# Weights from float64 with three instead of four word operations, and two factor groups with earlier due times

## The chip, the cores and the metric

The kernel runs on one core of a Trainium2 chip. The metric is the device time of one launch in microseconds. Before the change it is 1022.02 us, the median of three runs (1018.5 to 1025.15).

## The reference

Causal attention with a decay (4 batches, 8 heads, 576 positions, head dimension 64) gives 2304 tokens of width 512. Two layers of the same kind follow, each with a weight of 512 x 2048 and one of 2048 x 512 and a nonlinearity between them. Cut to what matters:

```python
scores = np.matmul(q, k.transpose(0, 1, 3, 2)) / np.sqrt(D) + decay      # causal, then softmax
x = attention @ v                                                        # (2304, 512)
h = x @ moe_w_in;  x = (h * np.clip(h + 3, 0, 6) / 6) @ moe_w_out
h = x @ moe2_w_in; g = np.maximum(h, 0) + np.log1p(np.exp(-np.abs(h)))
out = g @ moe2_w_out
```

The four weights reach the kernel as float64, since they are drawn as float64 and scaled. It reads each number as two 32-bit words and makes a float32 of it on the chip.

## The kernel before

**Stages.** Attention works on pairs of heads, 16 in all, for four batches. The first MoE starts on the first 512 tokens as soon as the first batch is through, so that attention and the first three token blocks of the first MoE (its matmuls are L1299 and L1362) run interleaved up to about 480 us. The last two token blocks follow, together with the making of the second MoE's weights and factors, up to about 645 us. The second MoE is done by a scheme with seven products in place of eight: phase A (L1415) makes its hidden layer in steps and sends it to DRAM, phase B (L1516) reads it back, makes factors of it (factors_g) and multiplies them with the second weight. At the border of the phases, about 825 to 860 us, both overlap.

**Weights.** There are 64 weight pieces of 128 x 512 numbers: 32 for the first MoE, whose result goes on to W tiles (L1035 on ScalarE takes the high part, L1036 on GpSimd the rest), and 32 for the second, most of which are written to DRAM as float32 and read again later. raw_weights brings one piece in by a DMA of 512 KB into a staging tile st, with low and high words side by side, and turns it into float32. Of the high word, seen as a float32, the exponent is shifted by a multiplication with 2 to the power -112 (conv0, on ScalarE at L1017, or on VectorE at L1016). The low word is shifted right by 29 (conv1, L1019). Then the high word shifted left by 3 is or-ed with that (conv2, L1020), and last the sign bit of the high word is or-ed in (conv3, L1023). The last three run on VectorE (DVE), and conv2 needs conv0.

**Order.** All operations are first recorded, each with the engine or engines that may do it (with a price in ns), what it reads and writes, and a due time `at` in us. Work.order then lists them: engine by engine it takes, of the operations that could start now, the one with the earliest due time. Where two engines may do an operation, it goes to the one that would be through with it first by the prices. So a removed operation moves nearly everything behind it by some places. The result is a fixed order for each engine; at run time an engine waits where an operand is late. Loads and stores stand in SP's order.

In factors_g and for the last weight group of the second MoE (weights2_in with p = 7), the due times counted from the phases' planned starts are:

```python
at = mb_at(t, 2 * d) - 7
weights2_in(1, p, ma_at(t, p, 1) + 4, 2)
```

Of the kernel before, what the change touches and what calls it, by code (L numbers as in the profile page):

```python
# [10 lines left out]
U32 = mybir.dt.uint32  # L11
ACTF = mybir.ActivationFunctionType
ALU = mybir.AluOpType
# [36 lines left out]
    pc=794.25,  # L50
# [21 lines left out]
    cvw=29.86,  # L72
# [33 lines left out]
class Work:  # L106
# [11 lines left out]
    def op(self, ways, fn=None, r=(), w=(), after=(), at=0.0, banks=(), hold=(), free=(), nbytes=0, name="", seq=None, from_=0.0, rows=1.0):  # L118


        o = Op()
        o.ways = [ways] if isinstance(ways, tuple) else list(ways)
        o.at, o.banks, o.hold, o.free, o.nbytes, o.name = at, list(banks), hold, free, nbytes, name
        o.deps, o.succ, o.est, o.eng = {}, [], 1000.0 * from_, None
        o.early, o.rows = self.mark, rows
        for b in o.banks:
            b.users += 1
        r, w = list(r) + o.banks, list(w)
        for t in r:
            if t in self.writer:  # L130
                o.deps[self.writer[t]] = 1
        for t in w:
            for d in [self.writer.get(t)] + self.readers.get(t, []):
                if d is not None:
                    o.deps.setdefault(d, 1)
        for t in after:
            for d in [self.writer.get(t)] + self.readers.get(t, []):
                if d is not None:
                    o.deps.setdefault(d, 0)
        if seq:  # L140
            if seq in self.writer:
                o.deps.setdefault(self.writer[seq], 0)
            self.writer[seq] = o
        for t in r:
            self.readers.setdefault(t, []).append(o)
        for t in w:
            self.writer[t] = o
            self.readers[t] = []
        self.ops.append(o)
        return o  # L150
# [123 lines left out]
def attention_two_moe_kernel(  # L274
# [18 lines left out]
    nc = tc.nc  # L293
# [15 lines left out]
    K = PLAN  # L309
# [27 lines left out]
    def act(n, psum, extra=0):  # L337
        return 0.833 * n + (50 if psum else 93) + 93 * extra

    def dve(n, fast=False, extra=0):  # L340
        return (0.52 if fast else 1.04) * n + 67 + 61 * extra
# [30 lines left out]
    def ma_at(t, p, x=0.0):  # L372

        return M2_0 + K["SA"] * (t * NPR + p + x)

    def mb_at(t, p, x=0.0):

        return MB + K["SB"] * (t * NPR + p + x)
# [606 lines left out]
    def words(i):  # L985

        return staging(i).bitcast(F32).rearrange("p n e -> p (n e)").rearrange("p (e n) -> p e n", e=2)

    def raw_weights(i, m, o, ft, at, dense=False):

        def load():
            dst = staging(i).rearrange("p n e -> p (n e)")
            if not wide:
                dst = dst.bitcast(F32)[:, 0:NC * P]
            if o == 0:
                dst = dst.rearrange("p (c f) -> p c f", c=NC)  # L1000
            nc.sync.dma_start(out=dst, in_=w_source(m, o, ft))

        dma(load, 8 * P * NC * P, w=[("stage", i), ("up", i)] + [("o", i, 0), ("o", i, 1)] * (i < 2), r=["m2"] * (i in (2, 3)), at=at - K["ldw"], name="loadw", from_=K["wfrom"])

        def up():
            return staging(i)[:, :, 1]

        def upf():
            return up().bitcast(F32)

        def low():
            return staging(i)[:, :, 0]

        n = NC * P
        if wide:
            op([("dve", dve(n, True), lambda: nc.vector.tensor_scalar(upf(), upf(), 2.0 ** -112, None, op0=ALU.mult), K["pc"]),  # L1016
                ("act", act(n, False), lambda: nc.scalar.activation(out=upf(), in_=upf(), func=ACTF.Copy, scale=2.0 ** -112))],  # L1017
               w=[("up", i)], at=at - K["cvw"], name="conv0")
            op(("dve", dve(n, True), lambda: nc.vector.tensor_scalar(low(), low(), 29, None, op0=ALU.logical_shift_right)), w=[("stage", i)], at=at - K["cvw"], name="conv1")  # L1019
            op(("dve", dve(n), lambda: nc.vector.scalar_tensor_tensor(  # L1020
                out=low(), in0=up(), scalar=3, in1=low(), op0=ALU.logical_shift_left, op1=ALU.bitwise_or,
            )), r=[("up", i)], w=[("stage", i)], at=at - K["cvw"], name="conv2")
            op(("dve", dve(n), lambda: nc.vector.scalar_tensor_tensor(  # L1023
                out=words(i)[:, 0].bitcast(U32) if dense else low(), in0=up(), scalar=0x80000000, in1=low(), op0=ALU.bitwise_and, op1=ALU.bitwise_or,
            )), r=[("up", i)], w=[("stage", i)] + [("up", i)] * dense, at=at - K["cvw"], name="conv3")

    def weights(o, ft, at):

# [115 lines left out]
    def weights2_in(o, p, at, i0):  # L1144

        def dst(z0, z1):
            return lambda s: unit_w(p).rearrange("p s z f -> p s (z f)")[:, s, z0 * 2 * P:z1 * 2 * P]

        weights2(o, p, at, [(a, b, dst(a, b), [("unit2" if o else "unit", p)], lambda: None) for a, b in ((0, 4), (4, 6), (6, 7))], i0)
# [319 lines left out]

    def factors_g(t, d):  # L1470

        at = mb_at(t, 2 * d) - 7
        i = (t * NPR // 2 + d) % 2
        raw = st[i].rearrange("p n e -> p (n e)").bitcast(F32)
        rv = raw.rearrange("p (r f h n) -> p r f h n", r=2, f=2, h=2)

        def cv():
            return (GT if i else BIG["XT"])[:, 0:8 * P].rearrange("p (z r n) -> p z r n", z=4, r=2)

        a0, a1 = t * NG, (t + 1) * NG  # L1480
        dma(lambda: nc.sync.dma_start(out=raw.rearrange("p (f s) -> p f s", f=4), in_=g_dram[4 * d:4 * d + 4, :, a0:a1].rearrange("f p s -> p f s")),
            16 * P * NG, r=[("gd", x, y) for x in range(a0 // NA, (a1 - 1) // NA + 1) for y in (2 * d, 2 * d + 1)],
            w=[("stage", i), ("up", i)], at=at - 8, name="loadg")
        A11, A12, A21, A22 = (rv[:, :, f, h] for h in range(2) for f in range(2))
        for x, (u, v, sub) in enumerate(((A21, A22, False), (0, A11, True), (A11, A21, True), (A12, 1, True))):
            def go(e, x=x, u=u, v=v, sub=sub):
                u, v = (cv()[:, y] if isinstance(y, int) else y for y in (u, v))
                e.tensor_tensor(cv()[:, x], u, v, op=ALU.subtract if sub else ALU.add)
            op(either(2 * P, go, 300), r=[("stage", i)] + [("C", i, y) for y in (u, v) if isinstance(y, int)], w=[("C", i, x)], at=at, name="gS")
        for n, z0, z1, src, rd in ((4 * P, 0, 2, lambda: rv[:, :, :, 0].rearrange("p r f n -> p f r n"), [("stage", i)]), (2 * P, 2, 3, lambda: A22, [("stage", i)]),  # L1490
                                   (8 * P, 3, 7, cv, [("C", i, x) for x in range(4)])):
            def dst(s, z0=z0, z1=z1):
                return gops(i, s)[:, z0:z1] if z1 > z0 + 1 else gops(i, s)[:, z0]

            op(("act", act(n, False), lambda src=src, dst=dst: nc.scalar.activation(out=dst(0), in_=src(), func=ACTF.Copy)),  # L1495
               r=rd, w=[("gf", i, z0, 0)], at=at + 1, name="gfh")

            def lo(e, src=src, dst=dst):
                e.tensor_tensor(dst(1), src(), dst(0).bitcast(F32), op=ALU.subtract)  # L1499
            op(either(n, lo, 300), r=rd + [("gf", i, z0, 0)], w=[("gf", i, z0, 1)], at=at + 1, name="gfl")  # L1500
# [107 lines left out]
    for t in range(NTA):  # L1608
        for p in range(NPR):
            step_a(t, p)  # L1610
            if p == NPR - 2 and t + 1 < NTA:
                factors_x(t + 1, ma_at(t, 1), 5.0)
            if t == NTA - 1:
                if p < 2:
                    freed([("xf", (t - 1) % 2, f) for f in AT[2]], [("unit2", p)])
                    freed([("unit", p)], [("gf", p, z0, s) for z0 in (0, 2, 3) for s in range(2)])
                else:
                    freed([("unit", p)], [("unit2", p)])
                if p < NPR - 1:
                    load_wo(p, ma_at(t, 0) if p < 2 else ma_at(t, p, 1))  # L1620
                else:
                    freed([("H", 0, q) for q in range(4)] + [("Yt", 0, 0), ("Yt", 0, 1)], [(x, i) for x in ("stage", "up") for i in (2, 3)])
                    weights2_in(1, p, ma_at(t, p, 1) + 4, 2)
    freed([("xt", 0), ("xt", 1)], [("C", 0, x) for x in range(4)])
    freed([("stage", 4), ("up", 4)], [("C", 1, x) for x in range(4)])
    freed([("stage", 5), ("up", 5)], [("u", x) for x in range(3)])
# [45 lines left out]
```

## Time and profile before

| | |
|---|---|
| median of three runs | 1022.02 us (1018.5 to 1025.15) |
| the profiled execution | 1020.33 us |
| its span, first to last instruction | 1018.3 us |
| TensorE (PE) busy | 978.4 us, 96% of the span |
| VectorE (DVE) busy | 838.2 us, 82% |
| ScalarE (ACT) busy | 599.8 us, 59% |
| GpSimd (POOL) busy | 256.4 us, 25% |
| mean granted TensorE clock | 0.993 |

A busy share is a mean over stages with different limits. PE's busy time is modelled from pipelined matmuls, so that a PE without idle time may still not be at its peak; its idle time is what tells of waits. The time outside the span, 2.0 us, belongs to the start and the end of the launch.

### The profile page before, as it was taken

The page shows a single profiled execution, that of the slowest core. Times are in us where ns is not written, and L with a number is a line of the kernel's source. Part 1 is how long each engine was busy: PE and PEld are TensorE (multiplying, and loading weights), DVE is VectorE, ACT ScalarE, POOL GpSimd, SP SyncE. Part 2 cuts the span into 40 slices and gives each one's busy share as a digit, 9 for nine tenths or more (in the row PEclk, how much of TensorE's full clock was granted, in tenths as well). Part 3 has the DMA queues.
Part 4 walks back from the last instruction along what each step waited for, and adds up shares of the span by engine and source line. Part 5 has one row for each costly group of instructions (what it writes and reads, how often), then busy time and mean ns, then how long its engine had stood idle before and what let it go on. Part 6 is the DMA issues. An engine that isn't in the chain of part 4 may idle for free.

```text
span 1018.3 us, 17717 instructions
## 1 busy us (share of the span) xinstructions
PE 978.4 (96%) x6116; PEld 850.4 (84%) x6116; DVE 838.2 (82%) x1662; ACT 599.8 (59%) x1309; POOL 256.4 (25%) x245
## 2 busy tenths in 40 slices
PE   8999999889999999999999999999999999999997
PEld 6566677668788888888888778899999999999997
DVE  8789979998999868998676878787787758888885
ACT  6899766877667557675443545665555544443442
POOL 2221241220000010000345744210010308454442
PEclk9999999999999999999999999999999999999999
DMA  6666553445545526443565660554324994444342
GB/s 138 168 143 157 136 145 94 122 134 153 145 141 144 135 66 177 118 138 104 180 209 178 225 212 21 163 169 141 140 105 164 340 359 134 126 146 145 112 125 77
DMA packets 192066, 153.47 MB, mean 151 GB/s; under 512 B 108220, under 2 KB 163932, under 8 KB 191080
## 3 DMA queue, kind: packets, MB, share of 16 engines
q1 hardware_dynamic: 191976, 152.34, 50.2%
q8 instruction: 48, 0.79, 0.3%
q14 instruction: 42, 0.34, 0.1%
HBM read 99.68 MB, written 52.47 MB: 149 GB/s over the span
## 4 chain that ended last, share of the span: by engine, by line
PE 67%; DVE 19%; issue 5%; ACT 3%; DMA 3%; POOL 2%; SPq 1%; DVEq 0%; POOLq 0%; ACTq 0%
PE bank L1516 16%; PE bank L1415 15%; PE bank L1299 13%; PE bank L1362 13%; PE bank L685 4%; PE bank L846 3%; PE bank L776 3%; DVE MX L1322 2%; DVE st L1020 2%; DVE GT L1341 1%; DVE st L1023 1%; DVE p L701 1%; DMA st<-in_moe_w_in_dram 1%; DVE KB L632 1%; DVE QA L632 1%
## 5 line engine op out<-in xcount | busy, mean ns | idle before, releaser
L1299 PE MATMUL bank<-MX,W 128*128 128x512 f32 x768 | 225.4, 406 | 4.1 <-DVE GT L1341 2.9
L1362 PE MATMUL bank<-MX,W 128*128 128x512 f32 (+1 forms) x688 | 188.4, 382 | 3.5 <-DVE MX L1322 3.5
L1299 PEld LDWEIGHTS bank<-MX,W 128*128 128x128 f32 x768 | 133.7, 191 | 26.6 <-DVE GT L1341 3.9
L1362 PEld LDWEIGHTS bank<-MX,W 128*128 128x128 f32 x688 | 121.6, 189 | 25.5 <-DVE MX L1322 4.1
L1516 PE MATMUL bank<-rW,rW 128*128 128x256 f32 x1134 | 138.6, 283 | 1.3 <-POOL rW L1139 0.9
L1516 PEld LDWEIGHTS bank<-rW,rW 128*128 128x128 f32 x1134 | 136.9, 191 | 2.1 <-POOL rW L1139 1.1
L1415 PE MATMUL bank<-XO,rW 128*128 128x288 f32 x672 | 92.7, 298 | 2.2 <-DVE HY L1433 1.6
L1415 PEld LDWEIGHTS bank<-XO,rW 128*128 128x128 f32 x672 | 90.3, 188 | 4.0 <-DVE HY L1433 2.3
L710 ACT ACTIVATE p<-p,stats 64x64 f32<-64x64 f32 (+4 forms) x130 | 72.2, 556 | 27.8 <-DVE stats L701 26.9
L1495 ACT ACTIVATE rW<-st 128x512 fp32r<-128x512 f32 (+1 forms) x72 | 36.9, 518 | 76.9 <-PE bank L1516 46.5
L1036 POOL TENSOR_TENSOR W<-st,W 128x512 fp32r<-128x512 f32 x24 | 34.9, 1456 | 159.8 <-ACT W L1035 133.8
L1339 ACT ACTIVATE GT<-bank,three 128x512 f32<-128x512 f32 x80 | 51.3, 643 | 39.6 <-DVE MX L1322 18.1
L1415 PE MATMUL bank<-MX,rW 128*128 128x288 f32 x480 | 70.2, 297 | 1.0 <-DVE HY L1433 1.0
L1415 PEld LDWEIGHTS bank<-MX,rW 128*128 128x128 f32 x480 | 65.7, 188 | 1.8 <-DVE HY L1433 1.4
L776 PE MATMUL bank<-ident,p 128*128 128x128 f32 x390 | 58.6, 275 | 8.3 <-DVE xs L861 4.4
L776 PEld LDWEIGHTS bank<-ident,p 128*128 128x128 f32 x390 | 46.2, 140 | 23.9 <-DVE xs L861 4.4
L581 POOL TENSOR_TENSOR V<-vr,V 128x640 fp32r<-128x640 f32 x10 | 17.2, 1718 | 189.3 <-ACT V L577 189.3
L811 ACT ACTIVATE pth<-bank 128x320 fp32r<-128x320 f32 (+2 forms) x100 | 42.3, 433 | 37.4 <-PE bank L776 26.3
L1322 DVE TENSOR_TENSOR MX<-GT,MX 128x512 fp32r<-128x512 f32 (+1 forms) x69 | 51.9, 757 | 13.0 <-ACT MX L1319 12.3
L1499 POOL TENSOR_TENSOR rW<-st,rW 128x256 fp32r<-128x256 f32 (+1 forms) x35 | 41.1, 1178 | 80.8 <-ACT rW L1495 66.5
L1341 DVE SCALAR_TENSOR_TENSOR GT<-GT,bank 128x512 f32<-128x512 f32 x80 | 49.8, 628 | 13.1 <-ACT GT L1339 12.5
L701 DVE CUSTOM_DVE_ANT_0 p<-bank,bar 64x64 f32<-64x64 f32 (+4 forms) x130 | 51.9, 421 | 6.4 <-PE bank L685 5.8
(220 smaller groups left out, 2102.8 us busy)
## 6 DMA issues: line engine op xcount, KB each, us to landing
st<-g_dram SPq DMA_DIRECT2D x36, 512.0 KB
st<-in_moe_w_out_dram SPq DMA_DIRECT2D x32, 512.0 KB
st<-in_moe_w_in_dram SPq DMA_DIRECT2D x30, 512.0 KB
wo_dram<-XO SPq DMA_DIRECT2D x49, 256.0 KB
g_dram<-HY SPq DMA_DIRECT2D x16, 576.0 KB
g_dram<-rBW SPq DMA_DIRECT2D x16, 576.0 KB
rW<-wo_dram SPq DMA_DIRECT2D x5, 1792.0 KB
wf_dram<-st SPq DMA_DIRECT2D x24, 256.0 KB
```

Of the source, the lines that this page charges most:

```text
L701: nc.vector.tensor_tensor_reduce(out=T["P"][par][ti][:r, a:c], in0=bank[bk.i][:r, o:o + c - a], in1=bar[:r, b0:b0 + c - a], op0=ALU.add, o ...
L710: nc.scalar.activation(out=pt, in_=pt, func=ACTF.Exp, scale=-1.0, bias=sv[:r, 0, ti:ti + 1], accum_out=sv[:r, 1, ti:ti + 1],)
L776: nc.tensor.transpose(acc[:, p0:p0 + P], T["P"][par][ti][:, k0:k0 + P], ident)
L811: nc.scalar.activation(out=place("PTH", j, ks, a, c), in_=src(), func=ACTF.Copy)
L1299: nc.tensor.matmul(bank[bk.i][:, 0:n], w[:, c], x[:, c, 0:n], start=(c == 0 and p == 0), stop=(c == NC - 1 and p == 2))
L1322: op(("dve", dve(n), lambda: nc.vector.tensor_tensor(t(glt), g, t(ght).bitcast(F32), op=ALU.subtract)), r=[("g", i), ("gh", i3)], w=[("gl" ...
L1339: op(("act", act(n, True, 1), lambda: nc.scalar.activation(out=g, in_=bank[bk.i][:, 0:n], func=ACTF.Relu, bias=three)), r=["three"], banks ...
L1341: op(("dve", dve(n), lambda: nc.vector.scalar_tensor_tensor(out=g, in0=g, scalar=6.0, in1=bank[bk.i][:, 0:n], op0=ALU.min, op1=ALU.mult)), ...
L1362: nc.tensor.matmul(bank[b][:, o:o + n], w[:, c * P:(c + 1) * P], x, start=(ft == 0 and p == 0 and o == 0), stop=(ft == NF - 1 and p == 2), ...
L1415: nc.tensor.matmul(bank[bks[b].i][:, 0:HA], wa[u][:, c], xa[v][:, c], start=(nm in ("P1", "P2", "P5") and c == 0 and y == 0), stop=(c == 1 ...
L1499: e.tensor_tensor(dst(1), src(), dst(0).bitcast(F32), op=ALU.subtract)
L1516: nc.tensor.matmul(bank[bks[b].i][:, o * 256:(o + 1) * 256], ga[u], wa[v], start=(p == 0 and o == 0 and y == 0), stop=(p == NPR - 1 and y ...
```

## The change

conv0 becomes one ScalarE activation with the function Prelu, the same scale and a slope of -(2 to the power 32) for negative numbers. A negative high word thus comes out positive, with an exponent that is higher by 32, and the shift left by 3 in conv2 carries that bit to the place of the sign. So conv3 goes, and conv2 writes the result where conv3 did. The choice of VectorE for conv0 goes too. At the border, the first two factor groups of phase B get a due time that is earlier by 18 us and the last weight group one that is later by 9 us.

```diff
--- before.py
+++ after.py
@@ -992,6 +992,7 @@
 
 
 
+
         def load():
             dst = staging(i).rearrange("p n e -> p (n e)")
             if not wide:
@@ -1013,16 +1014,12 @@
 
         n = NC * P
         if wide:
-            op([("dve", dve(n, True), lambda: nc.vector.tensor_scalar(upf(), upf(), 2.0 ** -112, None, op0=ALU.mult), K["pc"]),
-                ("act", act(n, False), lambda: nc.scalar.activation(out=upf(), in_=upf(), func=ACTF.Copy, scale=2.0 ** -112))],
+            op(("act", act(n, False), lambda: nc.scalar.activation(out=upf(), in_=upf(), func=ACTF.Prelu, scale=2.0 ** -112, alpha=-(2.0 ** 32))),
                w=[("up", i)], at=at - K["cvw"], name="conv0")
             op(("dve", dve(n, True), lambda: nc.vector.tensor_scalar(low(), low(), 29, None, op0=ALU.logical_shift_right)), w=[("stage", i)], at=at - K["cvw"], name="conv1")
             op(("dve", dve(n), lambda: nc.vector.scalar_tensor_tensor(
-                out=low(), in0=up(), scalar=3, in1=low(), op0=ALU.logical_shift_left, op1=ALU.bitwise_or,
-            )), r=[("up", i)], w=[("stage", i)], at=at - K["cvw"], name="conv2")
-            op(("dve", dve(n), lambda: nc.vector.scalar_tensor_tensor(
-                out=words(i)[:, 0].bitcast(U32) if dense else low(), in0=up(), scalar=0x80000000, in1=low(), op0=ALU.bitwise_and, op1=ALU.bitwise_or,
-            )), r=[("up", i)], w=[("stage", i)] + [("up", i)] * dense, at=at - K["cvw"], name="conv3")
+                out=words(i)[:, 0].bitcast(U32) if dense else low(), in0=up(), scalar=3, in1=low(), op0=ALU.logical_shift_left, op1=ALU.bitwise_or,
+            )), r=[("up", i)], w=[("stage", i)] + [("up", i)] * dense, at=at - K["cvw"], name="conv2")
 
     def weights(o, ft, at):
 
@@ -1469,7 +1466,7 @@
 
     def factors_g(t, d):
 
-        at = mb_at(t, 2 * d) - 7
+        at = mb_at(t, 2 * d) - (7 if t or d > 1 else 25)
         i = (t * NPR // 2 + d) % 2
         raw = st[i].rearrange("p n e -> p (n e)").bitcast(F32)
         rv = raw.rearrange("p (r f h n) -> p r f h n", r=2, f=2, h=2)
@@ -1620,7 +1617,7 @@
                     load_wo(p, ma_at(t, 0) if p < 2 else ma_at(t, p, 1))
                 else:
                     freed([("H", 0, q) for q in range(4)] + [("Yt", 0, 0), ("Yt", 0, 1)], [(x, i) for x in ("stage", "up") for i in (2, 3)])
-                    weights2_in(1, p, ma_at(t, p, 1) + 4, 2)
+                    weights2_in(1, p, ma_at(t, p, 1) + 13, 2)
     freed([("xt", 0), ("xt", 1)], [("C", 0, x) for x in range(4)])
     freed([("stage", 4), ("up", 4)], [("C", 1, x) for x in range(4)])
     freed([("stage", 5), ("up", 5)], [("u", x) for x in range(3)])
```

Lines of the changed kernel are lower by three from conv2 on (L1320 is L1317 there).

On DVE, at the last of the first MoE's 32 weight pieces (its tile is st_171; the rows around it are of attention, p and stats, and of the first MoE, GT and MX), before:

```order
L1019 TENSOR_SCALAR st_171<-st_171 128x512
L701 ISA p_152,stats_148<-bank_72,bar 64x64
L701 ISA stats_148 64x1
L1020 SCALAR_TENSOR_TENSOR st_171<-st_171 128x512
L1322 TENSOR_TENSOR MX<-GT,MX 128x512
L1023 SCALAR_TENSOR_TENSOR st_171<-st_171 128x512
L701 ISA p_153,stats_148<-bank_72,bar 128x192
L701 ISA stats_148 128x1
```

and now:

```order
L1019 TENSOR_SCALAR st_171<-st_171 128x512
L701 ISA p_153,stats_148<-bank_76,bar 128x192
L701 ISA stats_148 128x1
L701 ISA p_154,stats_148<-bank_71,bar 128x320
L701 ISA stats_148 128x1
L1020 SCALAR_TENSOR_TENSOR st_171<-st_171 128x512
L701 ISA p_155,stats_148<-bank_72,bar 128x448
L701 ISA stats_148 128x1
L1317 CAST MX<-GT 128x512
L816 TENSOR_TENSOR ptl_1439<-bank_75,pth_1435 128x320
L1319 TENSOR_TENSOR MX<-GT,MX 128x512
```

The row L1023 is gone, and between L1019 and L1020, and behind L1020, other rows stand. L1317 is one of the operations with two possible engines: it makes the high part of the first MoE's factor and stood on ACT more often before. In the whole order DVE has 64 rows of L1023 before and none now; 31 rows of L1320 before and 39 of L1317 now; 35 rows of L645 (a copy of a query or key factor, ACT or DVE) before and 39 now. On ACT the rows of L1017 are 63 before and 64 now.

On POOL at the border of the phases (XT and GT hold the sums of the factor groups, st_170 and st_171 the loaded groups, HY the last weight group), before:

```order
L1488 TENSOR_TENSOR XT<-st_170 128x256
L1488 TENSOR_TENSOR XT<-XT,st_170 128x256
L1499 TENSOR_TENSOR rW_5029<-st_171,rW_5029 128x256
L1107 TENSOR_TENSOR HY<-HY 128x256 x3
L1499 TENSOR_TENSOR rW_4877<-st_170,rW_4877 128x256
L1488 TENSOR_TENSOR GT<-st_171 128x256
L1488 TENSOR_TENSOR GT<-GT,st_171 128x256
L1488 TENSOR_TENSOR GT<-st_171,GT 128x256
L1139 TENSOR_TENSOR rW_5871<-HY,rW_5871 128x256
```

and now:

```order
L1485 TENSOR_TENSOR XT<-st_170 128x256
L1485 TENSOR_TENSOR XT<-XT,st_170 128x256
L1496 TENSOR_TENSOR rW_4973<-st_171,rW_4973 128x256
L1104 TENSOR_TENSOR HY<-HY 128x256 x3
L1496 TENSOR_TENSOR rW_4821<-st_170,rW_4821 128x256
L1485 TENSOR_TENSOR GT<-st_171 128x256
L1485 TENSOR_TENSOR GT<-GT,st_171 128x256
L1485 TENSOR_TENSOR GT<-st_171,GT 128x256
L1136 TENSOR_TENSOR rW_5809<-HY,rW_5809 128x256
```

The lines are lower by three and the tiles have other numbers; the operations stand in the same order. The same holds for every engine's order from the middle of phase A to the end: 98 rows of POOL, over 290 of ACT, over 430 of DVE, 125 DMAs of SP and all of phase B's matmuls. With the new due times at the border alone, and the four word operations as they were, the order of every engine is row by row that of before; with the three word operations alone it is row by row that of the change.

ACT's order holds two table loads before and two now, at the start and at the first softplus of phase A.

## Rows read from the trace of the kernel before

**Rows 1.** The page, first section: busy us, share of the span, instructions.

```profile
PE 978.4 (96%) x6116; PEld 850.4 (84%) x6116; DVE 838.2 (82%) x1662; ACT 599.8 (59%) x1309; POOL 256.4 (25%) x245
```

**Rows 2.** Stretches in us: length, busy us of each engine (instructions), granted clock, DMA.

```profile
0.00:50.00 50.00, 45.18 (x223) 29.71 (x224) 41.01 (x116) 36.67 (x101) 10.69 (x25) 1.00 0.69 155
50.00:100.00 50.00, 48.49 (x259) 33.06 (x258) 45.88 (x119) 46.60 (x118) 9.87 (x8) 1.00 0.65 151
100.00:250.00 150.00, 137.08 (x697) 105.94 (x695) 133.28 (x281) 108.28 (x239) 37.01 (x25) 0.98 0.48 127
250.00:475.00 225.00, 221.09 (x1205) 183.73 (x1204) 198.79 (x475) 151.53 (x351) 13.21 (x8) 1.00 0.47 133
475.00:645.00 170.00, 162.94 (x900) 138.89 (x899) 123.89 (x187) 77.03 (x167) 72.90 (x77) 0.99 0.53 167
```

**Rows 3.** PE's waits from 100 to 250 us: us in total, times, longest.

```profile
PE bank L776 <- DVE xs L861: 2.7, 2, 1.8
PE bank L1362 <- DVE MX L1322: 2.3, 1, 2.3
PE bank L776 <- DVE ptl L816: 2.2, 2, 1.2
```

**Rows 4.** The same stretches as Rows 2, instructions of L1023 alone: DVE busy.

```profile
0.00:50.00 50.00, 3.08 (x5) 1.00 0.69 155
50.00:100.00 50.00, 3.75 (x6) 1.00 0.65 151
100.00:250.00 150.00, 19.26 (x23) 0.98 0.48 127
250.00:475.00 225.00, 16.35 (x22) 1.00 0.47 133
475.00:645.00 170.00, 6.71 (x8) 0.99 0.53 167
```

**Rows 5.** Chain that ended last, by line: 100 to 250 us, then 250 to 475.

```profile
by line: PE bank L1299 15.4%; issue 9.8%; DVE st L1020 8.8%; PE bank L1362 8.7%; DVE st L1023 6.3%; DVE MX L1322 6.1%; PE bank L846 5.9%; PE bank L685 3.9%; PE bank L776 3.8%; DVE p L701 3.0%; DVE st L1019 2.7%; DVE KB L632 2.5%; DVE QA L63
...
by line: PE bank L1362 29.3%; PE bank L1299 27.4%; PE bank L685 9.9%; PE bank L776 9.0%; PE bank L846 5.0%; issue 3.7%; DVE xs L861 1.4%; DVE QA L632 1.3%; DVE KB L632 1.3%; DVE st L1020 1.2%; DVE GT L1341 0.9%; DVE MX L1281 0.8%; DVE p L70
```

**Rows 6.** The same chain, pieces from 500 to 650 us: start, us, what.

```profile
580.03 1.15 DVE st L1023
...
598.39 0.60 DVE HY L1023
...
614.44 0.61 DVE st L1023
```

**Rows 7.** L1023 over the span: count, ns least, median, most, first and last start.

```profile
L1023 DVE SCALAR_TENSOR_TENSOR st<-st x62: 630/689/1997, 22.2 to 647.7; 128x512 uint32<-128x512 uint32 x62
```

**Rows 8.** Around 187 us, DVE and POOL in order of time: start, us, engine, line.

```profile
187.42 1.80 DVE L1020 SCALAR_TENSOR_TENSOR st<-st 128x512 uint32<-128x512 uint32 x1
...
187.36 1.31 POOL L1036 TENSOR_TENSOR W<-st,W 128x512 fp32r<-128x512 f32 x1 [2.08 <-ACT W L1035]
```

**Rows 9.** Groups by form: count, busy us, mean ns, idle before and its releaser.

```profile
L1017 ACT ACTIVATE st<-st 128x512 f32<-128x512 f32 x61 | 41.1, 675 | 8.4 <-DMA st<-in_moe_w_in_dram 7.4 <-DMA st<-in_moe_w_out_dram 0.8
...
L1339 ACT ACTIVATE GT<-bank,three 128x512 f32<-128x512 f32 x64 | 43.8, 686 | 28.1 <-PE bank L1299 11.5 <-DVE MX L1322 10.1 <-DVE SB L1322 5.5
...
L1320 DVE CAST MX<-GT 128x512 fp32r<-128x512 f32 x28 | 12.9, 462 | 15.3 <-PE bank L1362 14.8
...
L645 DVE CAST QB<-QA 64x576 fp32r<-64x576 f32 x18 | 12.9, 718 | 0.1
```

**Rows 10.** The stretch from 225 to 235 us, columns as in Rows 2.

```profile
225.00:235.00 10.00, 7.72 (x26) 5.76 (x25) 7.65 (x21) 5.35 (x15) 2.81 (x2) 0.66 0.28 91
```

**Rows 11.** DVE's waits, 0 to 650 us: us in total, times, longest.

```profile
DVE st L1020 <- ACT st L1017: 3.4, 8, 1.1
```

**Rows 12.** PE's waits at the border, 822 to 860 us.

```profile
PE bank L1516 <- POOL rW L1139: 0.9, 1, 0.9
PE bank L1516 <- POOL rW L1499: 0.3, 1, 0.3
```

## Prediction

> **What bounds the kernel now.** I read the busy shares first [rows 1]: PE is busy 96% of the span, so that a gain can come only out of the few places where PE waits or runs slowly. The table of stretches [rows 2] tells where these are. From 250 to 475 us PE is idle for 225 - 221.1 = 3.9 us, from 475 to 645 us for 7.1 us. From 100 to 250 us it is idle for 150 - 137.1 = 12.9 us, and there DVE is busy 133.3 of 150 us, while ACT is busy 108.3 and POOL 37.0. The longest waits of PE in this stretch all end with DVE [rows 3]. So from 100 to 250 us DVE is a second bound beside PE: it makes weights for the first MoE, the softmax's sums and the MoE's factors, all in one queue. In the first 100 us ACT is the fuller engine of its second half (46.6 of 50 us), and PE is idle for 4.8 and 1.5 us.
>
> The clock comes next. In the ten microseconds from 225 us the granted clock is 0.66 on the mean [rows 10], that is some 6.8 us at 1.2 GHz in place of 2.4 and about 3.4 us of PE's work lost; PE had been busy 7.7 of those 10 us. From 250 us on DVE is still full (198.8 of 225), but PE hardly waits, so there DVE has just enough room.
>
> **The change, part by part.** *conv3 goes.* It has 64 instructions and takes 3.1 + 3.8 + 19.3 + 16.4 + 6.7 us up to 645 us [rows 4], with 0.7 us behind that 49.8 us in all. The median of one is 0.689 us, the longest 1.997 [rows 7]; 64 x 0.689 = 44.1 us is its own work. The rest, 5.7 us, is waiting inside the instruction: at 187.42 us the sister operation L1020 took 1.80 us while a POOL instruction of 1.31 us had begun 0.06 us before [rows 8]. That waiting need not vanish with conv3, for the instruction that takes its place in the queue can meet the same POOL instruction. The Trainium skill states this as a rule (SBUF — State Buffer, section "SBUF: two separate sides"): an operation of VectorE with two SBUF inputs and one of GpSimd share a pair of ports, whoever starts first holds it for the whole instruction, and the other is blocked. The trace agrees, 1.31 us of POOL making 1.80 of 0.69. By the rule I would count conv3 at its own 0.689 us, without it at its mean of 0.77; I use the median, which the rows give anyhow.
>
> What is this worth in time? *From 100 to 250 us* L1023 has 6.3% of the chain that ended last [rows 5], 9.5 us of its 19.3. Its own work there is 23 x 0.689 = 15.8 us, so I take 9.5 x 15.8 / 19.3 = 7.7 us. Below, the bound is nothing: the chain may run over another engine just as long. Above, it is PE's whole idle time of 12.9 us. The low clock follows a stretch in which PE waits; with fewer waits it may stay away. That is 0 to 3.4 us; I take the half, 1.7. *Up to 100 us* 11 instructions go (6.8 us), but L1023 is on no long piece of the chain there and ACT is full: 0 to 2 us, taken as 0.5. *From 250 to 475 us* the line is missing among those of at least 0.8% of the chain [rows 5], so it has less than 1.8 us; 0 to PE's 3.9, taken as 1.0. *From 475 us on* it has three pieces, 1.15 + 0.60 + 0.61 = 2.4 us [rows 6]; 0 to 7.1 us, taken as 2.0.
>
> *What DVE gets back.* In the new order it has eight more of the L1320 kind (0.462 us) and four more of the L645 kind (0.718 us) [rows 9]: 3.7 + 2.9 = 6.6 us, so that it is relieved of 44.1 - 6.6 = 37.5 us. They were handed to it because it is free earlier, mostly behind 250 us, and ACT is rid of them. At the share of the chain that L1023 has over the span (7.7 + 0.5 + 1.0 + 2.0 of 44.1, a quarter) they cost 1.7 us if they land as badly, nothing if they stand in gaps, and I take 0.5.
>
> *conv0 as Prelu.* 63 of the 64 stand on ACT already, at 0.675 us. Prelu is not in the trace; the nearest rows are this copy with a scale and the Relu at L1339, 0.686 us for the same width from PSUM with a bias per partition [rows 9]. I take no difference; 64 x 0.011 = 0.7 us more of ACT's time would be hidden behind PE from 100 us on. Since ACT's order holds two table loads as before, none is added. The one conv0 that leaves DVE is within the numbers above.
>
> *The wait that stays.* conv2 still waits for conv0; it did so eight times for 3.4 us, 1.1 at most [rows 11]. What is behind it in DVE's queue are the softmax's minima and PE's factors. The new order puts other work between conv1 and conv2 at the place shown, which gives ACT the same time that it had. Nothing is taken for it; the fourth rival below prices it.
>
> *The border.* The new due times move nothing: the orders are the same there, on all engines. With that the term is nothing. PE's waits at the border are 0.9 and 0.3 us [rows 12], so even a perfect border would bring 1.2 us. That part of the change therefore does not do what its words say.
>
> The sum: 7.7 + 1.7 + 0.5 + 1.0 + 2.0 - 0.5 = 12.4 us off the profiled execution's 1020.33 us (span 1018.3), 1007.9 us. That execution is 1.7 us below the median of the runs, 1022.02; on the scale of the median it is 1009.6, said as 1010 us.
>
> **The rivals.** Every case has one uncertainty in common: the removal reshuffles the order of five engines from the first weight on, by the planner's prices, and PE's small waits fall elsewhere. I give it 4 us to either side.
>
> *The forecast*, conv3's part of the chain goes and most of it is not replaced: 1010 us, 1004 to 1016, chance 0.50.
>
> *DVE's load, not the chain, is what counts.* Where an engine is 89% busy, taking 15.8 us out of it lets everything behind it move up, and PE's idle time from 100 to 250 us goes altogether, with the low clock: 12.9 + 3.4, and 4 us from elsewhere, 20 us, 1002 us. For it speaks that all long waits of PE end with DVE; against it, that DVE itself waits there for 16.7 us. Chance 0.18.
>
> *Another wait takes the place.* PE and DVE hand work to and fro, and softmax's chain over PE, DVE and ACT keeps its length; then only the pieces behind 475 us and half of the clock are won, 4 us: 1018 us. For it: from 250 to 475 us PE is 98% busy, and issue time alone has 9.8% of the chain from 100 to 250 us [rows 5]. Chance 0.25.
>
> *Slower: DVE stands still at conv2.* DVE takes its instructions in order. With conv3 gone it comes to conv2 sooner, while ACT reaches conv0 no sooner. If each of the 23 weights from 100 to 250 us met the longest wait seen, 1.1 us, that were 25.3 us against the 15.8 saved, 9.5 us on the wrong side, 1032 us. It decides from a mean wait of 0.69 us per weight on, conv3's own length; the mean now is 3.4 / 64 = 0.05 us. Chance 0.07.
>
> **How the numbers follow.** About 1%, 10.2 us, is what a measurement of this kernel can tell from no change; the bounds are 1011.8 and 1032.2 us. Of the forecast's 0.50 I put 0.35 below 1011.8, of the second case all 0.18, of the others nearly nothing: faster 0.54 with 0.01 from the third. Slower has 0.05, the greater part of the last case; 0.41 remains for the same. The range goes from 1001, with half of the second case below 1002 (0.08 left out), to 1020, which leaves out the last case and a fifth of the third (0.12).
>
> **What would show it.** In the new profile: no L1023; DVE's busy sum of 838 us lower by 35 to 45; in the stretch that before took from 100 to 250 us, PE's idle time down from 12.9 to about 5 us; the first MoE's last first-block matmuls earlier by 8 to 10 us, and nearly no further gain up to 475 us. A mean clock of 1.00 there shows the clock's term. Phases A and B should be as long as now, within 1 us, and the border as it is. The waits of conv2 for L1017 should stay under 8 us in all. The prediction is wrong if those waits grow, if ACT's conv0 is clearly longer than 0.69 us, or if PE's idle time appears again in another stage, between 250 and 645 us, where the order was reshuffled as well.

## The result: 1.1% faster

The change takes 1009.22 us, the median of four runs (1006.66 to 1012.72). Its ratio to before is 0.9885, with a 95% interval from 0.9855 to 0.9914. (One execution of before, 2.9 ms long, is left out of that.) In a later set of runs on another chip it was 0.9897 [0.9867, 0.9928]. The profiled execution took 1006.66 us with a span of 1004.7, 13.7 us less than the one before.

The page's first section and the stretches of the changed kernel (columns as in Rows 1 and 2):

```profile
PE 972.6 (97%) x6116; PEld 847.3 (84%) x6116; DVE 801.8 (80%) x1615; ACT 590.1 (59%) x1295; POOL 249.2 (25%) x242
```

```profile
0.00:50.00 50.00, 45.46 (x226) 30.18 (x227) 38.36 (x115) 38.35 (x104) 11.94 (x26) 1.00 0.70 156
50.00:100.00 50.00, 46.47 (x251) 31.47 (x250) 43.66 (x111) 44.42 (x115) 11.36 (x10) 1.00 0.68 171
100.00:250.00 150.00, 144.73 (x758) 113.61 (x758) 126.47 (x284) 112.90 (x253) 34.31 (x24) 1.00 0.48 128
250.00:475.00 225.00, 222.92 (x1221) 185.90 (x1220) 185.04 (x452) 143.40 (x333) 11.70 (x8) 1.00 0.48 134
```

DVE's busy sum fell from 838.2 to 801.8 us [rows 1]. From 100 to 250 us PE is idle for 150 - 144.7 = 5.3 us in place of 12.9 [rows 2], it does 758 matmuls there in place of 697, and the granted clock is 1.00, that is 2.4 GHz throughout, in place of 0.98.

To see where the time came off, one follows marks through both profiles: the last matmul of attention (L846), the last of the first MoE (L1362, now L1359), the first and last of phase A (L1415, now L1412). Each row gives count, ns (least, median, most), first and last start. Before:

```profile
L846 PE MATMUL bank<-ptl,V x120: 220/292/338, 158.8 to 483.1; 128*64 128x320 f32 x60, 128*64 128x128 f32 x20, 128*64 128x256 f32 x20, 128*64 128x192 f32 x20
L1362 PE MATMUL bank<-SB,BL x4: 276/278/281, 640.4 to 642.9; 128*128 128x256 f32 x4
L1415 PE MATMUL bank<-XO,rW x672: 290/297/404, 643.0 to 783.0; 128*128 128x288 f32 x168
L1415 PE MATMUL bank<-MX,rW x480: 290/297/404, 689.6 to 833.1; 128*128 128x288 f32 x160
```

The changed kernel:

```profile
L846 PE MATMUL bank<-ptl,V x120: 220/292/338, 157.0 to 471.0; 128*64 128x320 f32 x60, 128*64 128x128 f32 x20, 128*64 128x256 f32 x20, 128*64 128x192 f32 x20
L1359 PE MATMUL bank<-SB,BL x4: 276/280/281, 625.7 to 628.2; 128*128 128x256 f32 x4
L1412 PE MATMUL bank<-XO,rW x672: 290/297/406, 628.3 to 769.2; 128*128 128x288 f32 x168
L1412 PE MATMUL bank<-MX,rW x480: 289/297/400, 675.8 to 819.6; 128*128 128x288 f32 x160
```

Attention ends 12.1 us sooner, the first MoE another 2.6 us (14.7 in all), and phase A gives 1.2 us back: it lasts 819.6 - 628.3 = 191.3 us where it lasted 190.1.

The chain that ended last, from 100 to 250 us, shows what is late next:

```profile
by line: PE bank L1296 20.7%; PE bank L1359 14.9%; issue 9.2%; PE bank L846 8.4%; PE bank L685 5.9%; PE bank L776 5.4%; DMA st<-in_moe_w_in_dram 4.0%; DVE MX L1319 3.0%; DMA st<-in_moe_w_out_dram 2.9%; DVE st L1020 2.7%; POOL W L1033 2.0%; 
```

Beside [rows 5], L1020 fell from 8.8 to 2.7% and L1023's 6.3% is gone. In their place stand PE's own matmuls and the loads of weights into the two staging tiles, 6.9% or 10.4 us; before, no load stood on this chain in that stretch. It looks as if the pieces are made fast enough now that the chain goes over their loads; no run tests this.

### The profile page after: what moved, and what is told of

Same layout as the page of the kernel before. It is cut to its first block, busy times and chain, and to the rows that moved or that the text cites. A ratio compares the mean times of both kernels' runs of the same rounds, so it can differ in the third digit from the quotient of the medians.

```text
span 1004.7 us, 17646 instructions
## 1 busy us (share of the span) xinstructions
PE 972.6 (97%) x6116; PEld 847.3 (84%) x6116; DVE 801.8 (80%) x1615; ACT 590.1 (59%) x1295; POOL 249.2 (25%) x242
## 4 chain that ended last, share of the span: by engine, by line
PE 69%; DVE 16%; issue 4%; DMA 4%; ACT 2%; POOL 2%; SPq 1%; DVEq 0%; POOLq 0%; ACTq 0%
PE bank L1513 16%; PE bank L1296 14%; PE bank L1412 14%; PE bank L1359 13%; PE bank L685 5%; PE bank L846 4%; PE bank L776 4%; DVE MX L1319 2%; DVE GT L1338 1%; DMA st<-in_moe_w_in_dram 1%; DVE p L701 1%; DVE st L1020 1%; SPq L535 1%; DMA st<-in_moe_w_out_dram 1%; DVE KB L632 1%
## 5 line engine op out<-in xcount | busy, mean ns | idle before, releaser
L1359 PE MATMUL bank<-MX,W 128*128 128x512 f32 (+1 forms) x688 | 186.3, 380 | 0.0
L1359 PEld LDWEIGHTS bank<-MX,W 128*128 128x128 f32 x688 | 121.5, 188 | 22.1 <-DVE MX L1319 0.3
L1412 PE MATMUL bank<-XO,rW 128*128 128x288 f32 x672 | 92.8, 298 | 3.0 <-DVE HY L1430 1.2
L1412 PEld LDWEIGHTS bank<-XO,rW 128*128 128x128 f32 x672 | 90.3, 188 | 4.9 <-DVE rBW L1430 1.8
L1412 PE MATMUL bank<-MX,rW 128*128 128x288 f32 x480 | 70.2, 297 | 1.3 <-DVE HY L1430 1.0
L1412 PEld LDWEIGHTS bank<-MX,rW 128*128 128x128 f32 x480 | 65.8, 188 | 2.1 <-DVE HY L1430 1.2
L1338 DVE SCALAR_TENSOR_TENSOR GT<-GT,bank 128x512 f32<-128x512 f32 x80 | 49.9, 629 | 14.3 <-ACT GT L1336 13.3
L776 PEld LDWEIGHTS bank<-ident,p 128*128 128x128 f32 x390 | 46.6, 140 | 14.7 <-DVE ptl L816 1.6
```

The source lines that it names most:

```text
L776: nc.tensor.transpose(acc[:, p0:p0 + P], T["P"][par][ti][:, k0:k0 + P], ident)
L1338: op(("dve", dve(n), lambda: nc.vector.scalar_tensor_tensor(out=g, in0=g, scalar=6.0, in1=bank[bk.i][:, 0:n], op0=ALU.min, op1=ALU.mult)), ...
L1359: nc.tensor.matmul(bank[b][:, o:o + n], w[:, c * P:(c + 1) * P], x, start=(ft == 0 and p == 0 and o == 0), stop=(ft == NF - 1 and p == 2), ...
L1412: nc.tensor.matmul(bank[bks[b].i][:, 0:HA], wa[u][:, c], xa[v][:, c], start=(nm in ("P1", "P2", "P5") and c == 0 and y == 0), stop=(c == 1 ...
```

## Experiments

Times are medians; ratios are to before, with 95% intervals, each from runs on the same chip, and can differ a little from the quotient of the medians. The edits are shown shortened, with names in place of operands.

**The old order, without the work.** conv3 stays in the plan with its price and emits nothing. The order is row by row that of before, apart from the rows of L1023 and one conv0.

```diff
-op([("dve", dve(n, True), tensor_scalar ...), ("act", ..., Copy ...)], name="conv0")
+op([("dve", dve(n, True), prelu), ("act", ..., prelu)], name="conv0")        # both emit the Prelu on ACT
+op(("dve", dve(n), (up << 3) | low -> final place), name="conv2")
-op(("dve", dve(n), (up & sign) | low), name="conv3")
+op(("dve", dve(n), lambda: None), name="conv3")
```

> The order of before on every engine, planned with conv3 at its full price, but conv3 emits nothing: conv0 is the Prelu, conv2 writes the final float32. Theory (DVE's time at conv3 stood on the chain, mostly between 100 and 250 us): most of the gain is there without any new order, 8 to 12 us below before, about 1010 to 1015 us. Rival (the gain comes from the newly listed order, which happens to suit PE better): at most 4 us below before, 1018 us or more.

1004.26 us, ratio 0.9827 [0.9797, 0.9857]. The gain is there without any new order, and it is greater than expected, greater than the change's own. The rival, that the new order brought the gain, falls. This profile helps further below: PE's matmuls follow in the very order of before, so that one and the same matmul can be looked up in both.

**The work back in the new order.**

```diff
 conv2: (up << 3) | low -> o
+       (o & 0) | o -> o        # in the same recorded operation, price unchanged
```

> The order of the changed kernel on every engine, but each conv2 is followed by a DVE instruction of the size of conv3 that changes nothing and that the planner does not know of: 64 x 0.69 = 44 us of DVE work are back. Theory: the gain is gone, 1020 to 1028 us, more than before rather than less, since the order has no room for it. Rival (the order brought the gain): within 4 us of the changed kernel, 1005 to 1013 us.

1053.29 us, ratio 1.0303 [1.0269, 1.0338]: far above what I expected. The 44 us of work cost 44 us. The stretches of this kernel's profile show a part of the reason:

```profile
0.00:25.00 25.00, 21.72 (x84) 15.64 (x85) 18.01 (x48) 12.43 (x31) 5.30 (x21) 0.80 0.62 130
100.00:250.00 150.00, 131.84 (x625) 98.73 (x624) 127.52 (x260) 99.09 (x219) 37.14 (x25) 0.93 0.42 114
```

From 100 to 250 us PE is idle for 18.2 us, and its clock is 0.93 on the mean. Over the span of 1054.7 us the mean clock is 0.980, some 21 us of PE's work lost, against 1 us in the changed kernel's profile (0.999). That is 20 of the 50.0 us between these two spans, and 5 of the 20 stand in the first 25 us, whose clock differs between runs of one and the same program (see the end). Over all four runs of each, the mean clocks are 0.984 and 0.996, which makes it some 13 of the 44 us. The rest must be waiting: each of PE's factors comes later by what stands in front of it. That is argued, not measured wait by wait.

**One half of the pieces each.** raw_weights takes the three operations for one MoE's pieces and keeps the four of before for the other's, planned as they are.

```diff
+if m == 0:      # the next run: if m == 1
     three operations
+else:
+    four operations
```

> The three word operations for the first MoE's 32 pieces alone, which are made up to about 230 us; the second MoE's 32 keep four. Theory: the first 250 us hold 9 of the 13 to 14 us, so 1012 to 1015 us. Rival (what counts is DVE's load over the whole attention, so each half of the pieces is worth half): 1016 to 1017 us.

1012.84 us, ratio 0.9907 [0.9882, 0.9933].

> The three word operations for the second MoE's 32 pieces alone, made from about 230 to 645 us; the first MoE's 32 keep four. Theory: 3 to 5 us, 1018 to 1020 us. Rival (each half is worth half): 1016 to 1017 us.

1020.84 us, ratio 0.9987 [0.9971, 1.0003]. This is just above the theory's range. So the first MoE's 32 pieces, made up to about 230 us, are worth 9.5 us of before's 1022.36, and the others 1.5, which is not clear of nothing. The rival of equal halves falls.

**A fifth operation.**

```diff
 conv3
+op(("dve", dve(n), (o & 0) | o -> o), name="conv4")
```

> Before with a fifth word operation for each piece, of the size of conv3 and planned for, that changes nothing: the dose in the other direction. Theory (DVE's load before 290 us sets the time): about as much on top as the change took off, 10 to 18 us, 1032 to 1040 us. Rival (PE's own work is the bound and before was only unluckily ordered): within 5 us of before, 1017 to 1027 us.

1034.73 us, ratio 1.0147 [1.0116, 1.0177]: 13.6 us on top of 1021.12, as much as the change takes off. Planned, one operation per piece is worth 13 us in either direction, not the 44 us of the unplanned one.

**Without conv1.** In this run and the one after it conv2 takes the high word a second time in place of the shifted low word, so that the weights are not the right numbers.

```diff
-op(("dve", dve(n, True), low >> 29), name="conv1")
-conv2: (up << 3) | low
+conv2: (up << 3) | up
```

> The changed kernel without conv1, so that a weight takes two operations; the low three bits and part of the mantissa are not computed as they should. 64 x 0.43 = 27 us of DVE work go. Theory with PE near its bound: PE is idle for only 5.3 us from 100 to 250 us now, so 2 to 5 us are left to gain, 1004 to 1007 us. Rival (DVE's load goes on setting the time at the same rate as from four to three operations, 13.6 us for 44): 8 us, 1001 us.

1010.87 us, ratio 0.9907 [0.9881, 0.9933]. Nothing is gained by 27 us less on DVE, and the time lies above the theory's range and the rival's. But every step here was listed anew; so the same was done without a new order:

```diff
 old order, conv3 emits nothing
-op(("dve", dve(n, True), low >> 29), name="conv1")
+op(("dve", dve(n, True), lambda: None), name="conv1")
-conv2: (up << 3) | low
+conv2: (up << 3) | up
```

> The kernel with the old order and nothing emitted for conv3, and now nothing for conv1 either (the low bits of the weights are not as they should be): 27 us of DVE work less at no change of order. Theory (PE is near its bound, little is left for DVE to hold up): 0 to 3 us below the 1004.3 us of the old order, 1001 to 1004 us. Rival (DVE's load still sets the time and only the new listing hid it in the run without conv1): 996 to 999 us.

1001.74 us, ratio 0.9819 [0.9794, 0.9843], against 0.9827 for the same order with conv1: little is left, as the theory had it. With the fifth operation, before, the change and this run one sees a knee: 13 us for the fifth, 13 to 18 for the fourth, 2.5 at most for conv1. The stretch from 100 to 250 us shows where it lies; the rows are of five operations, of the old order without conv3, and of that without conv1 too:

```profile
100.00:250.00 150.00, 136.69 (x670) 103.78 (x671) 141.98 (x301) 109.53 (x241) 35.59 (x25) 0.95 0.47 125
100.00:250.00 150.00, 144.13 (x748) 113.78 (x746) 123.17 (x281) 115.89 (x259) 36.80 (x26) 0.99 0.53 139
100.00:250.00 150.00, 144.91 (x752) 114.42 (x751) 115.89 (x261) 116.47 (x263) 35.71 (x26) 0.99 0.52 140
```

PE is idle there for 13.3 us with five operations, for 12.9 with four, and for 5.9 and 5.1 in the last two rows. The low clock takes another 0.05 x 150 = 7.5 us of PE's work with five, 3.0 with four [rows 2], and 1.5 in the last two. Together that is 21, 16, 7 and 7 us: conv1's 27 us on DVE hardly bring PE anything there any more. (These stretches are of one length in time, and hold less of the work in the slower kernels, so they show the knee and not its whole size.)

**Is the old order better than the change's?** Both once more, side by side.

> The changed kernel once more, side by side with the next run, to settle whether the old order is really better. Theory (it is, by what the first MoE's last token blocks and phase A lose in the new order, 3.1 and 1.2 us in the profiles): about 0.9885 of before, 1008 to 1010 us. Rival (the 5 us were the runs' scatter): within 2 us of the next run.

> The old order with nothing emitted for conv3, once more. Theory: 3 to 6 us below the changed kernel, 1003 to 1006 us, about 0.983 of before. Rival: within 2 us of the changed kernel.

1011.58 us and 1006.96 us, ratios 0.9897 [0.9867, 0.9928] and 0.9860 [0.9832, 0.9888]. Both are 1 to 2 us above what was expected; the difference is within the theory's 3 to 6. It is 4.6 us here, where both ran on one chip, and 5.0 us between the first runs of the two, which were on different chips. The intervals against before overlap, but only one of these six runs of the change (1007.49 us) is faster than any of the five of the old order. The marks in the profiles agree: from the last matmul of attention to the last of the first MoE the change takes 628.2 - 471.0 = 157.2 us and the old order 625.1 - 470.2 = 154.9; phase A takes 191.3 and 815.2 - 625.2 = 190.0 us. The old order's marks:

```profile
L846 PE MATMUL bank<-ptl,V x120: 220/292/338, 156.6 to 470.2; 128*64 128x320 f32 x60, 128*64 128x128 f32 x20, 128*64 128x256 f32 x20, 128*64 128x192 f32 x20
L1363 PE MATMUL bank<-SB,BL x4: 276/280/281, 622.7 to 625.1; 128*128 128x256 f32 x4
L1416 PE MATMUL bank<-XO,rW x672: 289/297/404, 625.2 to 765.2; 128*128 128x288 f32 x168
L1416 PE MATMUL bank<-MX,rW x480: 290/297/402, 671.8 to 815.2; 128*128 128x288 f32 x160
```

The same two lengths, in us, from every profile of these two programs and of three runs that follow:

| profile | attention's end to the first MoE's end | phase A |
|---|---|---|
| the change | 157.2 | 191.3 |
| the change, once more | 631.5 - 473.7 = 157.8 | 823.2 - 631.7 = 191.5 |
| the old order | 154.9 | 190.0 |
| the old order, once more | 630.7 - 474.4 = 156.3 | 820.6 - 630.8 = 189.8 |
| the third sum on POOL | 633.2 - 476.3 = 156.9 | 824.1 - 633.4 = 190.7 |
| more left to POOL | 629.4 - 473.6 = 155.8 | 821.9 - 629.5 = 192.4 |
| conv2 priced at two | 624.7 - 469.0 = 155.7 | 815.4 - 624.8 = 190.6 |

In phase A the two orders lie 1.3 and 1.7 us apart, and one program's profiles 0.2. In the first MoE they lie 2.3 and 1.5 us apart, but one program's profiles up to 1.4: in the second of the old order the clock is 0.91 from 525 to 545 us. That makes 3.6 and 3.2 us behind attention.

PE's waits in the last 60 us of the first MoE, the changed kernel from 567 to 632 us (us in total, times, longest):

```profile
PE bank L1296 <- DVE GT L1338: 1.9, 4, 0.7
PE bank L1359 <- ACT SB L1316: 0.6, 1, 0.6
PE bank L1359 <- DVE SB L1319: 0.4, 1, 0.4
```

and the old order without conv3, from 567 to 629 us:

```profile
PE bank L1300 <- DVE GT L1342: 0.6, 1, 0.6
```

So the new order makes PE wait for DVE there. One thing that DVE has more of in it is a sum of the second MoE's first factors, 1.9 us, which POOL had before. The next run gives it back to POOL; little else moves.

```diff
-op(either(n, go), r=key + ["m2"] + pace(i), ...)
+op(either(n, go)[1:] if (t, i) == (0, 2) else either(n, go), r=key + ["m2"] + pace(i), ...)   # [1:]: POOL alone
```

> The changed kernel, but the third sum of the second MoE's first factors (1.9 us on DVE at 602 us, ahead of the first MoE's factors) is left to POOL, as it was before; nearly nothing else moves in the order. Theory (the new order gives DVE this sum because DVE looks free, and PE then waits for its factors around 604 to 609 us): 1.5 to 3 us below the changed kernel's 1009.2 us, 1006 to 1008 us. Rival (the 5 us by which the old order is better lie spread over many places): within 1 us of the changed kernel.

1008.65 us, ratio 0.9883 [0.9860, 0.9906], as the change. The theory of this one sum falls. What DVE won it lost again in part, as two rows from that place show, POOL's and then DVE's (start, us, engine, line):

```profile
608.68 1.89 POOL L1218 TENSOR_TENSOR XT<-XO,XT 128x576 f32<-128x576 f32 x1 [0.69 <-DVE XO L1213]
```

```profile
609.26 1.59 DVE L1317 CAST MX<-GT 128x512 fp32r<-128x512 f32 x1
```

The copy took 1.59 us, beside 0.462 on the mean [rows 9], and ended 0.28 us after POOL's sum. Then the planner was made to leave more of all such work to POOL:

```diff
-    pv=600,
+    pv=800,
```

> The changed kernel, where the planner charges DVE 800 ns more in place of 600 ns for the sums and differences that POOL could do as well (second MoE's weights and factors). The order is the changed kernel's up to about 575 us; behind that DVE has 11 sums of the x factors in place of 15, as many as before had, and POOL five in place of one. Theory (of the 4 to 5 us by which the old order is better, the larger part is such work that DVE got for being free, ahead of the first MoE's factors): 3 to 5 us below the changed kernel, 0.985 to 0.987 of before, about 1006 us. Rival (it is the placement of all engines' rows, not DVE's share): within 1.5 us of the changed kernel, 1009 to 1011 us.

1007.86 us, ratio 0.9886 [0.9867, 0.9905]: again the change's ratio. (The time is below the rival's 1009 to 1011 us, but before took only 1019.03 us on this chip; the theory's 0.985 to 0.987 was not reached.) In its profile the first MoE's rest is 1.4 us shorter than in the change's, phase A 1.1 us longer. So DVE's share of these sums is not what costs 4 to 5 us. That most of it lies behind attention is shown; what it is stays open.

**Room in the plan.** conv2 is priced at two of itself, so that the planner lists for the old load, but in an order of its own.

```diff
-op(("dve", dve(n), ...), name="conv2")
+op(("dve", 2 * dve(n), ...), name="conv2")
```

> The changed kernel with conv2 priced at two of itself, so that the planner lists as if DVE had the old load, in an order of its own. Theory (a listing that leaves DVE some room is better than one that fills it): near the old order's 1004.3 us, 1002 to 1007 us. Rival (the old order is better by chance, since the due times around were set for it): as the changed kernel, 1008 to 1011 us.

1006.79 us, ratio 0.9858 [0.9831, 0.9886]. It is within the theory's range, but the interval takes in the change's 0.9885; it is a hint that room helps, no proof. The planner hands DVE less in it: DVE is busy for 792.4 us, as in the old order (791.9), against 801.8 in the change. The version to keep is the old order with an empty conv3: it was 18.1 and 14.4 us below before, and 5.0 and 4.6 us below the change. Between it and this last version (14.5 us below before) the runs do not decide.

## Why the prediction was right

The forecast was 1010 us, and 1009.22 came out; of 12.4 us counted on the profiled execution 13.7 came. By its steps:

*conv3 up to 250 us*, with the clock: 7.7 + 1.7 + 0.5 = 9.9 us forecast. The old order without conv3 measures the removal alone. This is one matmul of PE's, before and in the old order (start, us):

```profile
250.12 0.87 PE L1299 MATMUL bank<-MX,W 128*128 128x512 f32 x3
```

```profile
240.67 0.89 PE L1300 MATMUL bank<-MX,W 128*128 128x512 f32 x3
```

It comes 9.5 us sooner. The halves agree on the size: 9.5 us for the pieces made up to 230 us. In the change PE's idle time went from 12.9 to 5.3 us, where about 5 was said. The step was right, in mechanism and size, and it is the removal itself.

*The clock.* The stretch with 0.66 [rows 10] is gone from the change's profile. Over the runs it is less clear: beside the six later runs of the change (0.993 to 1.000, 0.995 on the mean) stand 11 of before on the same chip with 0.987 to 0.998 and 0.992. That is some 5 and 8 us lost, a gain of 3 to 4 where 1.7 was taken, and only an estimate, since the ranges overlap.

*Behind 250 us* the removal was sized too small. From 250 us to the end of attention it brings 12.9 - 9.5 = 3.4 us in the old order (483.1 against 470.2 us), where 1.0 was taken with 0 to 3.9 as bounds. From there to the end of the first MoE it brings 159.8 - 154.9 = 4.9, where 2.0 was taken with 0 to 7.1; some 1.7 of these belong to the clock, 0.99 before [rows 2] and 1.00 in the old order. *The new order* was taken at 0.5 us for what DVE gets back, and else only as a scatter of 4 us to either side. It costs 0.8 us up to the end of attention (471.0 against 470.2), 2.3 in the first MoE and 1.3 in phase A, which was to be the same within 1 us: 4.4 us in these profiles.

So 5.3 us were missing on the one side, and about 4 on the other. That the total fits as well as it does is luck in this part; the range held both.

*What DVE gets back* was counted as 6.6 us of work; the busy sum fell by 36.4 us, and 37.5 was the count. In the old order, where DVE gets nothing back, it fell by 838.2 - 791.9 = 46.3 us.

*conv0 as Prelu* costs nothing, as taken: 676 ns in place of 675. The row of the changed kernel (count, busy us, mean ns, idle before):

```profile
L1017 ACT ACTIVATE st<-st 128x512 f32<-128x512 f32 x62 | 41.8, 676 | 7.0 <-DMA st<-in_moe_w_in_dram 4.3 <-DMA st<-in_moe_w_out_dram 2.3
```

*The wait of conv2 for conv0*, the rival on the slower side, did not grow in sum [rows 11]:

```profile
DVE st L1020 <- ACT st L1017: 3.4, 6, 1.3
```

That is 0.05 us per piece as before, far from the 0.69 from which it would decide. *The border* is as it was; PE's waits there, from 808 to 846 us, against [rows 12]:

```profile
PE bank L1513 <- POOL rW L1136: 0.8, 1, 0.8
PE bank L1513 <- POOL rW L1496: 0.3, 1, 0.3
```

and phase B lasts from its first to its last matmul 999.2 - 812.5 = 186.7 us, before 186.8. Since the orders are the same there, the new due times did nothing; no run tests them alone.

Of the rivals, *another wait takes the place* would have given 1018 us, and *DVE's load counts* 1002. The fifth operation, at 13.6 us, speaks for the load up to the knee: before stood on its steep side, and the change stands close to the flat one. The old order without conv3 came to 1004 and 1007, between the forecast's number and that rival's. But the rival's mechanism, that PE's idle time from 100 to 250 us goes altogether, did not show: 5.9 us are left there.

## What to carry to other kernels

Where one engine of a pair is full and the other waits for it, price a removed operation by its share of the chain in that stretch, with the second engine's idle time there as the upper bound; the bound of 12.9 us held, and 9.5 came. Count the smaller terms with care as well: behind 250 us 3.0 us were taken and 8.3 came. Adding 44 us of work cost 13 us when the plan knew of them and 44 when it did not. Where a planner lists the work, an edit has two effects, the work and the new order: keep the old order with an empty operation, and each can be measured by itself. Look at the order before giving a moved due time any value; here two moved not one row.

## What the runs showed of the hardware

Work that PE waits for can cost twice. With the unplanned operation, PE's idle time from 100 to 250 us rose from 5.3 to 18.2 us, and the mean clock fell from 1.00 to 0.93 in the same stretch, which is 10.5 us of PE's work.

An instruction of DVE can take longer beside one of POOL. A word operation of 0.69 us took 1.80 [rows 8], and a copy of 0.46 us took 1.59 while POOL's sum of 1.89 us ran.

The clock's first stretch differs between runs of one and the same program. In the first profile of the old order the first 25 us have a clock of 1.00, in the second 0.80, which is 2 * 0.20 * 25 = 10 us at 1.2 GHz in place of 2.4, and 5 us of PE's work; attention ends 474.4 - 470.2 = 4.2 us later.

```profile
0.00:25.00 25.00, 20.76 (x110) 15.56 (x111) 20.09 (x54) 15.75 (x40) 5.30 (x21) 1.00 0.68 138
```

```profile
0.00:25.00 25.00, 21.89 (x84) 15.86 (x84) 18.05 (x48) 12.44 (x31) 5.30 (x21) 0.80 0.61 130
```

The change's two profiles have 1.00 and 0.86 there, and attention ends 2.7 us apart. A comparison of two single profiles can thus be off by 4 to 5 us for that alone. The lengths between marks that both pass later are steadier, but not free of it: they differ by up to 1.4 us for one program.
